# Planning the bit moves of pairs 6 and 7 at every other step of a fused attention and MLP kernel

## The chip, the cores and the metric

One core of a Trainium2 chip. The metric is the device time of one launch in microseconds (us). In a profile, times count from the first instruction of the span; a span is somewhat shorter than the device time (302.6 us for a run of 304.4 us). In the lines of a profile PE is TensorE, PEld its weight loads, DVE VectorE, ACT ScalarE and POOL GpSimd; L470 is line 470 of the kernel, x4 a count of instructions, and <- in brackets names what ended a wait.

## The reference, cut to what matters

```python
# attention with a hash mask: q, k, v are [4, 8, 768, 64], proj is [64, 6]
q_bits = (q @ proj > 0); k_bits = (k @ proj > 0)      # 6 bits per row
mask = bucket(q_bits) == bucket(k_bits)               # attend only within a bucket
attn = softmax(where(mask, q @ k.T / 8, -1e9))
x = (attn @ v)                                        # to [3072, 512]
# then an MLP: w_in [512, 2048], w_out [2048, 512]
h = x @ w_in
out = (h * sigmoid(h)) @ w_out
```

## The kernel before: the parts that matter

The kernel walks the 32 heads as 16 pairs, in 288 steps (nine score tiles per head), and slips the MLP of one batch element between the attention steps of the next. The bits of a pair are laid under its q and k rows, in tiles `QKA` (first head) and `QKB` (second head), so that a score matmul adds the mask by itself. The bits are computed for two pairs at once (`proj_unit`) and then moved to their rows (`bits_unit`), by VectorE for pairs up to 7 and by DMA above:

```python
def bits_unit(pairs, i, par):               # i: which pair, par: 0 = QKA, 1 = QKB
    p = pairs[i]
    t, r0 = ((QKA[p % NSL], 64), (QKB[p % NSL], 0))[par]
    if p > 7:
        ...                                 # DMAs
        return
    for n in range(2):                      # q rows, then k rows
        c = 32 * (2 * i + n)
        r = slice(c, c + NR)                # 13 partitions of the bits tile
        dst = t[r0 : r0 + NR, n * S : (n + 1) * S]...
        if n == 1 and par == 1:
            nc.vector.tensor_scalar(out=dst, in0=bits[pairs][r, :, 0:CB], ...)
        else:
            nc.vector.tensor_copy(out=dst, in_=bits[pairs][r, :, 0:CB])
```

So a group of moves is two VectorE instructions, and pairs 6 and 7 have four groups. The other user of VectorE that counts here is `g`, the last step of the first MLP matmul. Three PSUM tiles with the tag "m" rotate; a tile is free again when its `g` is done:

```python
hp = ps.tile([P, f, n], F32, tag="m", name="h_ps", bufs=3)
...                                         # four matmuls into hp
th = thp.tile([P, f, n], F32, tag="th", name="th")
nc.scalar.activation(out=th, in_=hp, func=AF.Tanh, scale=0.5)
after.append(lambda: nc.vector.scalar_tensor_tensor(    # g = (th + 1) * hp
    out=g[ci][...], in0=th, scalar=1.0, in1=hp, op0=ALU.add, op1=ALU.mult))
```

Each step issues the waiting `g` first, then what is planned for the step (`plan(step, fn)`), then MLP units and attention:

```python
for w in range(NW):
    flush()                                 # the g of the step before
    for fn in at.pop(w, []):
        fn()                                # planned units, such as bits_unit
    ...                                     # MLP units, av(w), score(w + LEAD)
```

Of the kernel before, what the change touches and what calls it, by code (L numbers as in the profile page):

```python
# [17 lines left out]
def kernel(  # L18
# [67 lines left out]
    def load_blocks(p):  # L86
        b, h0 = p // 4, 2 * (p % 4)
        for n, src in (("q", q), ("k", k)):
            t = ld.tile([P, NG, 32], F32, tag=f"ld{n}", name=f"{n}_blk")
            for j in range(4):  # L90
                i, half = divmod(j, 2)
                nc.sync.dma_start(  # L92
                    out=t[32 * j : 32 * j + 32],
                    in_=src[b, h0 + i].rearrange("(r g) d -> r g d", r=32)
                    [:, :, 32 * half : 32 * half + 32])
            qk_sb[p, n] = t

    def load_v(p, heads=slice(0, 2)):
        b, h0 = p // 4, 2 * (p % 4)
        if p not in v_sb:  # L100
            v_sb[p] = vld.tile([P, 2, NJ * D], F32, tag="ldv", name="v_sb")
        nc.sync.dma_start(
            out=v_sb[p][:, heads],
            in_=v[b, h0 : h0 + 2][heads].rearrange("h (p t) d -> p h (t d)", p=P))
# [135 lines left out]
    def block_unit(p, n):  # L240
        if n == 0:
            qk32[p] = t32.tile([P, 2 * S], F32, tag="qk32", name="qk32")

        dst = qk32[p][:, n * S : (n + 1) * S].rearrange(
            "p (t r a) -> p a t r", t=NJ, r=32, a=4)
        nc.vector.transpose(out=dst, in_=qk_sb[p, "qk"[n]])  # L246

    def cast_unit(p, par):
        sl = p % NSL
        dst, rows = ((QKA[sl], slice(0, 64)), (QKB[sl], slice(64, 128)))[par]  # L250
        nc.gpsimd.tensor_scalar(out=dst[rows, :], in0=qk32[p][rows, :],  # L251
                                scalar1=CS, scalar2=1.0,
                                op0=ALU.mult, op1=ALU.mult)

    def v_unit(p, heads=(0, 1)):
        for i in heads:
            h = 2 * p + i
            vv, vs = VV[h % NVS], VS[p % (NVS // 2)]
            src = v_sb[p][:, i, :].rearrange("p (t d) -> p t d", d=D)
            nc.gpsimd.tensor_copy(out=vv[:, :, 0:D], in_=src)  # L260
            sa = nrm.tile([P, 3, D], F32, tag="vsa", name="vsa")
            nc.gpsimd.tensor_tensor(out=sa, in0=src[:, 0:3], in1=src[:, 3:6], op=ALU.add)  # L262
            sb = nrm.tile([P, D], F32, tag="vsb", name="vsb")
            nc.gpsimd.tensor_tensor(out=sb, in0=sa[:, 0], in1=sa[:, 1], op=ALU.add)
            nc.gpsimd.tensor_tensor(out=vs[:, i, 0:D], in0=sb, in1=sa[:, 2], op=ALU.add)
# [4 lines left out]
    def proj_unit(*pairs):  # L270



        bt = btp.tile([P, 3, CB + 2], F16, tag="bits", name="bits")
        bps = []
        for c0, w in ((0, 512), (512, S - 512)):
            bp = ps.tile([P, 512], F32, tag="m", name="bp_ps", bufs=3)
            for i, p in enumerate(pairs):
                for n in range(2):
                    c = 32 * (2 * i + n)  # L280
                    nc.tensor.matmul(bp[c : c + 32, 0:w], pw[:, 0:32],  # L281
                                     qk32[p][:, n * S + c0 : n * S + c0 + w],
                                     start=True, stop=True)
            bps.append((bp, c0, w))
        r = slice(0, 64 * len(pairs))
        for bp, c0, w in bps:
            nc.vector.tensor_scalar(out=bt[r, c0 // CB : (c0 + w) // CB, 0:CB],
                                    in0=bp[r, 0:w].rearrange("d (x c) -> d x c", c=CB),
                                    scalar1=sc[r, 0:1], scalar2=sc[r, 1:2],
                                    op0=ALU.is_gt, op1=ALU.subtract)  # L290
        bits[pairs] = bt
# [30 lines left out]
    def bits_unit(pairs, i, par):  # L322
# [5 lines that stand above are left out]
            o = par * (NBIT + 1)  # L328
            for n in range(2):
                r = 32 * (2 * i + n) + o  # L330
                nc.sync.dma_start(out=t[r0 + o : r0 + o + NBIT, n * S : (n + 1) * S]
                                  .rearrange("d (x c) -> d x c", c=CB),
                                  in_=bits[pairs][r : r + NBIT, :, 0:CB])
            return
        for n in range(2):
            c = 32 * (2 * i + n)
            r = slice(c, c + NR)
            dst = t[r0 : r0 + NR, n * S : (n + 1) * S].rearrange("d (x c) -> d x c", c=CB)
            if n == 1 and par == 1:
                nc.vector.tensor_scalar(out=dst, in0=bits[pairs][r, :, 0:CB],  # L340
                                        scalar1=sc[r, 2:3], scalar2=None, op0=ALU.mult)
            else:
                nc.vector.tensor_copy(out=dst, in_=bits[pairs][r, :, 0:CB])  # L343
# [228 lines left out]
    def plan(w, fn):  # L572
        at.setdefault(w, []).append(fn)
# [35 lines left out]
    for Q in range(2, NQUAD):  # L609
        w0 = (Q - 1) * QST  # L610
        for i in range(4 if Q > 2 else 0):
            w1 = w0 + (5, 9, 12, 15)[i]
            plan(w1, lambda Q=Q, i=i: block_unit(2 * Q + i // 2, i % 2))
            if i % 2:
                for par in range(2):
                    plan(w1, lambda p=2 * Q + i // 2, par=par: cast_unit(p, par))
        wp = w0 + {2: 24, 3: 21}.get(Q, 20)
        plan(wp, lambda Q=Q: proj_unit(2 * Q, 2 * Q + 1))
        for i in range(4):
            plan(wp + (i if Q < 4 else 0),  # L620
                 lambda Q=Q, i=i: bits_unit((2 * Q, 2 * Q + 1), i // 2, i % 2))
        for i in range(2):
            plan(w0 + 5 + i, lambda p=2 * Q + i: load_v(p))
            for j in range(2):
                plan(w0 + 18 + 9 * i + 2 * j, lambda p=2 * Q + i, j=j: v_unit(p, (j,)))
            if Q + 1 < NQUAD:
                plan(w0 + (28 if Q == 3 else 8) + i, lambda p=2 * Q + 2 + i: load_blocks(p))
# [74 lines left out]
```

## Time and profile before

| kernel before | value |
|---|---|
| device time, median of 4 runs (lowest, highest) | 304.20 us (304.14, 304.9) |
| span of the profiled run | 302.6 us |
| busy: TensorE, ScalarE, VectorE, GpSimd | 98%, 69%, 59%, 42% |
| visible waits of h_ps matmuls for g, all together | 0.8 us, one wait |

TensorE sets the time. The question for any change of VectorE's order is therefore whether TensorE waits for VectorE anywhere, and for how long.

### The profile page before, as it was taken

The page shows a single profiled execution, that of the slowest core. Times are in us where ns is not written, and L with a number is a line of the kernel's source. Part 1 is how long each engine was busy: PE and PEld are TensorE (multiplying, and loading weights), DVE is VectorE, ACT ScalarE, POOL GpSimd, SP SyncE. Part 2 cuts the span into 40 slices and gives each one's busy share as a digit, 9 for nine tenths or more (in the row PEclk, how much of TensorE's full clock was granted, in tenths as well). Part 3 has the DMA queues.
Part 4 walks back from the last instruction along what each step waited for, and adds up shares of the span by engine and source line. Part 5 has one row for each costly group of instructions (what it writes and reads, how often), then busy time and mean ns, then how long its engine had stood idle before and what let it go on. Part 6 is the DMA issues. An engine that isn't in the chain of part 4 may idle for free.

```text
span 302.6 us, 7181 instructions
## 1 busy us (share of the span) xinstructions
PE 297.0 (98%) x2710; PEld 175.1 (58%) x2710; DVE 180.0 (59%) x344; ACT 210.1 (69%) x392; POOL 128.2 (42%) x203
## 2 busy tenths in 40 slices
PE   8999999998999999999999999999999999999996
PEld 3676755545665665555565665555566654446653
DVE  5797938899568454854695434954443442764332
ACT  5987989988887686878886766878877732452300
POOL 6589999386618561845149411765111100000000
PEclk9999999999999999999999999999999999999999
DMA  7999998999979828744068146011022003001112
GB/s 202 245 248 215 156 145 122 217 180 166 145 161 153 131 74 229 124 97 134 3 126 139 51 63 203 2 40 32 2 61 63 4 34 95 35 2 69 37 66 73
DMA packets 103170, 32.87 MB, mean 109 GB/s; under 512 B 90656, under 2 KB 100192, under 8 KB 103136
## 3 DMA queue, kind: packets, MB, share of 16 engines
q1 hardware_dynamic: 98752, 28.22, 43.3%
q0 software_dynamic: 4224, 4.19, 9.0%
q8 instruction: 21, 0.34, 0.5%
q14 instruction: 13, 0.11, 0.1%
q10 hardware_dynamic: 160, 0.00, 0.0%
HBM read 27.27 MB, written 6.29 MB: 111 GB/s over the span
## 4 chain that ended last, share of the span: by engine, by line
PE 89%; DVE 5%; DMA 2%; issue 1%; SPq 1%; ACT 1%; POOL 0%; DVEq 0%; ACTq 0%; POOLq 0%
PE o_ps L496 26%; PE h_ps L461 24%; PE s_ps L366 18%; PE o_ps L398 11%; PE bp_ps L281 3%; DMA v_sb<-in_v_dram 2%; PE tp_ps L185 2%; DVE g L470 2%; PE o_ps L482 1%; PE warm_ps L125 1%; SPq L92 1%; DVE qka L343 1%; PE bp_ps L225 1%; DVE qk L246 1%; PE tp_ps L198 0%
## 5 line engine op out<-in xcount | busy, mean ns | idle before, releaser
L369 ACT ACTIVATE u<-s_ps 128x512 f16<-128x512 f32 x288 | 157.0, 606 | 38.7 <-PE s_ps L366 38.3
L470 DVE SCALAR_TENSOR_TENSOR g<-th,h_ps 128x512 f16<-128x512 f32 x96 | 65.5, 686 | 74.8 <-ACT th L468 74.7
L461 PE MATMUL h_ps<-xT,win 128*128 128x512 f16 (+1 forms) x512 | 98.4, 325 | 0.8 <-DVE g L470 0.8
L398 PEld LDWEIGHTS <-u 128*128 128x128 f16 x1152 | 68.1, 98 | 42.2 <-ACT u L369 8.4
L496 PE MATMUL o_ps<-wout,g 128*128 128x512 f16 x368 | 91.6, 379 | 0.0
L468 ACT ACTIVATE th<-h_ps 128x512 f32<-128x512 f32 x96 | 57.9, 603 | 36.6 <-PE h_ps L461 33.9
L398 PE MATMUL o_ps<-vv,u 128*128 128x65 f16 x1152 | 82.6, 194 | 0.6 <-ACT u L369 0.4
L461 PEld LDWEIGHTS <-win 128*128 128x128 f16 x512 | 49.8, 98 | 31.4 <-issue 1.0
L418 POOL TENSOR_TENSOR x_pr<-osum,rec 128x384 f16<-128x384 f32 x23 | 19.0, 826 | 89.3 <-DVE rec L417 88.9
L496 PEld LDWEIGHTS <-g 128*128 128x128 f16 x368 | 35.8, 98 | 33.6
L366 PE MATMUL s_ps<-qka 71*128 71x512 f16 x192 | 52.7, 327 | 0.2 <-DVE qka L238 0.2
L366 PE MATMUL s_ps<-qkb 128*128 128x512 f16 x192 | 52.6, 326 | 0.0
L251 POOL TENSOR_SCALAR qka<-qk 64x1536 f16<-64x1536 f32 x15 | 22.0, 1466 | 11.4 <-DVE qk L246 5.6
L501 DVE TENSOR_SCALAR osb<-o_ps 128x512 f32<-128x512 f32 x23 | 15.9, 691 | 15.0 <-PE o_ps L496 15.0
L251 POOL TENSOR_SCALAR qkb<-qk 64x1536 f16<-64x1536 f32 x15 | 22.1, 1471 | 1.2
L262 POOL TENSOR_TENSOR vsa<-v_sb 128x192 f32<-128x192 f32 x32 | 19.0, 592 | 0.0
L260 POOL CAST vv<-v_sb 128x384 f16<-128x384 f32 x32 | 16.2, 507 | 0.9 <-DMA v_sb<-in_v_dram 0.5
L246 DVE STREAM_TRANSPOSE qk<-k_blk 128x768 f32<-128x768 f32 x10 | 15.8, 1582 | 0.3 <-issue 0.3
L246 DVE STREAM_TRANSPOSE qk<-q_blk 128x768 f32<-128x768 f32 x10 | 15.9, 1591 | 0.0
L366 PEld LDWEIGHTS <-qka 71*128 71x128 f16 x192 | 15.5, 97 | 0.8 <-ACT qka L238 0.7
L366 PEld LDWEIGHTS <-qkb 128*128 128x128 f16 x192 | 15.4, 97 | 0.0
L412 DVE TENSOR_TENSOR osum<-o_ps,vsum 128x390 f32<-128x390 f32 x23 | 13.0, 565 | 2.3
(70 smaller groups left out, 163.0 us busy)
## 6 DMA issues: line engine op xcount, KB each, us to landing
out_dram<-osb SPq DMA_DIRECT2D x23, 256.0 KB
v_sb<-in_v_dram SPq DMA_DIRECT2D x15, 384.0 KB
q_blk<-in_q_dram SPq DMA_DIRECT2D x40, 96.0 KB
k_blk<-in_k_dram SPq DMA_DIRECT2D x40, 96.0 KB
win<-in_moe_w_in_dram POOLq DMA_DIRECT2D x4, 512.0 KB, 6.6
wout<-in_moe_w_out_dram POOLq DMA_DIRECT2D x4, 512.0 KB, 6.9
q_sb<-in_q_dram SPq DMA_DIRECT2D x5, 384.0 KB
k_sb<-in_k_dram SPq DMA_DIRECT2D x5, 384.0 KB
```

The lines of the kernel that those rows point to most:

```text
L246: nc.vector.transpose(out=dst, in_=qk_sb[p, "qk"[n]])
L251: nc.gpsimd.tensor_scalar(out=dst[rows, :], in0=qk32[p][rows, :], scalar1=CS, scalar2=1.0, op0=ALU.mult, op1=ALU.mult)
L260: nc.gpsimd.tensor_copy(out=vv[:, :, 0:D], in_=src)
L262: nc.gpsimd.tensor_tensor(out=sa, in0=src[:, 0:3], in1=src[:, 3:6], op=ALU.add)
L366: nc.tensor.matmul(sp[:, o0 : o0 + n], t[rows, S + jt * P : S + (jt + 1) * P], t[rows, c0 : c0 + n], start=True, stop=True)
L369: nc.scalar.activation(out=u, in_=sp, func=AF.Exp, scale=ESC)
L398: nc.tensor.matmul(o_ps[h][:, c0 // P + i, :], u[:, o0 + i * P : o0 + (i + 1) * P], vv[:, jt, :], start=(not direct(h) and w % NU == 0 and ...
L418: (nc.vector if direct(h) else nc.gpsimd).tensor_tensor(out=x_pr[p][:, :, par * D : (par + 1) * D], in0=o[:, 0:NJ, 0:D], in1=rec[:, :, Non ...
L461: nc.tensor.matmul(hp[:, j, :], w_in16[:, dt, ft * P : (ft + 1) * P], xT[4 * b + dt][:, c0 : c0 + n], start=(dt == 0), stop=(dt == NDT - 1))
L468: nc.scalar.activation(out=th, in_=hp, func=AF.Tanh, scale=0.5)
L470: after.append(lambda: nc.vector.scalar_tensor_tensor(out=g[ci][:, grp * f : (grp + 1) * f, :], in0=th, scalar=1.0, in1=hp, op0=ALU.add, o ...
L496: nc.tensor.matmul(o2[tt], g[ci][:, ft, ct * P : (ct + 1) * P], w_out16[:, ft, :], start=(ft == 0), stop=(ft == NFT - 1))
```

## The change

The intent is to let the `g` instructions of the MLP pass between the moves. Only the steps of the four groups of pairs 6 and 7 (Q = 3) change, from 93, 94, 95, 96 to 93, 95, 97, 99:

```diff
         for i in range(4):
-            plan(wp + (i if Q < 4 else 0),
+            plan(wp + {2: i, 3: 2 * i}.get(Q, 0),
                  lambda Q=Q, i=i: bits_unit((2 * Q, 2 * Q + 1), i // 2, i % 2))
```

## The prediction

> **What bounds the kernel now.** I read the summary of the page first, then the sum of waits of the whole run, then the chain that ended last around the steps that the change touches, and last the order in time of TensorE and VectorE there.
>
> ```profile
> PE 297.0 (98%) x2710; PEld 175.1 (58%) x2710; DVE 180.0 (59%) x344; ACT 210.1 (69%) x392; POOL 128.2 (42%) x203
> PE h_ps L461 <- DVE g L470: 0.8, 1, 0.8
> ```
>
> The first line is the busy time of each engine: TensorE is busy for 297.0 of 302.6 us. The second is from the list of waits: of all the matmuls that write the hidden tile h_ps of the second half (the MLP), exactly one waits visibly for VectorE, once, for 0.8 us. So a change that only reorders VectorE can win little more than that one gap. The other VectorE work is mostly beside TensorE.
>
> The chain that ended last shows where the gap is. Columns: start, length, what.
>
> ```profile
> 67.09 1.18 DVE bits L287 x2
> ...
> 68.30 0.54 DVE qka L343
> ...
> 68.86 0.54 DVE qka L343
> ...
> 69.42 0.54 DVE qkb L343
> ...
> 69.97 0.60 DVE qkb L340
> ...
> 70.60 0.69 DVE g L470
> ...
> 71.32 0.54 DVE qka L343
> ...
> 73.00 0.61 DVE qkb L340
> ...
> 73.64 0.70 DVE g L470
> 74.33 0.04 issue
> 74.38 1.02 PE h_ps L461 x4
> ```
>
> The reader is to see that from 67.09 to 74.33 us the chain runs through VectorE: eight bit moves (two groups of four) with one g between and one behind them, and that it then passes to TensorE, where it stays, but for short waits near 97 us, to the last output tile. L343 and L340 are the two forms of a bit move; these are the moves of pairs 6 and 7, the ones the change replans. L470 makes g from th and h_ps and so frees the PSUM tile of h_ps.
>
> TensorE and VectorE in order of time, in the same place (start, length, what, idle before):
>
> ```profile
> 71.83 1.03 PE L461 MATMUL h_ps<-xT,win 128*128 128x512 f16 x4
> ...
> 73.16 0.38 PE L366 MATMUL s_ps<-qkb 128*128 128x256 f16 x2
> 74.38 1.02 PE L461 MATMUL h_ps<-xT,win 128*128 128x512 f16 x4 [0.84 <-DVE g L470]
> ...
> 75.97 1.04 PE L461 MATMUL h_ps<-xT,win 128*128 128x512 f16 x4
> ```
> ```profile
> 74.24 0.22 DVE L411 COPY vsum<-o_ps 128x65 f32<-128x65 f32 x1
> ...
> 75.27 1.84 DVE L470 SCALAR_TENSOR_TENSOR g<-th,h_ps 128x512 f16<-128x512 f32 x3
> 77.68 0.69 DVE L470 SCALAR_TENSOR_TENSOR g<-th,h_ps 128x512 f16<-128x512 f32 x1 [0.57 <-ACT th L468]
> ```
>
> I number the h_ps tiles by their start on TensorE: H1 67.51, H2 69.09, H3 70.63, H4 71.83, H5 74.38, H6 75.97, H7 77.56. The pool has three buffers, so H5 needs the g of H2. That g was runnable at 70.75 (its tanh starts at 70.15 and takes 0.60), but VectorE takes its work in order and did it only at 73.64 to 74.33. H5 starts 0.05 later. A score pair such as the one at 73.16 is normally followed 0.22 us later by the next tile (69.95 to 70.07 to 70.29 and so on), so H5 should have started at 73.38: by starts the stall is 74.38 - 73.38 = 1.00 us; the 0.84 is counted from the modelled end of the matmul. H6 lost a further 0.06: due 0.22 after the score at 75.69, it started at 75.97, 0.05 after the first g of the three at 75.27. In all 1.06 us is there to be won.
>
> **What the Trainium skill says.** "PSUM — Partial Sum Buffer", section "Engine vs sequencer instructions": the queues of VectorE, ScalarE and GpSimd are strictly first in, first out, and matmuls start and complete in program order. The trace agrees: H2's g, runnable at 70.75, stands behind four moves until 73.64, and no TensorE work passes H5. "Perfetto Trace Analysis", section "Matmuls": independent groups should rotate through PSUM banks so that the evacuation of one overlaps the matmuls of the next. Here they do, with three tiles, and the rotation breaks just once, by 1.00 us. "VectorE: DVE Perf Modes", section "Two Vector instructions with no wait between them": in its model, an instruction whose operands start at another group of 32 partitions than the last ones waits for all earlier ones. The trace agrees: g after g starts every 0.59 us though each takes 0.69 (59.11 and three in 1.84), while a g after a bit move, or a move after a g, starts 0.02 to 0.03 us after its end. So each g that the change puts between moves loses about 0.1 us of overlap that a row of g has.
>
> **The change part by part.** It adds and removes no instruction. For pairs 6 and 7 the four groups of moves (two instructions each) are planned at steps 93, 95, 97, 99 in place of 93 to 96. The built program shows TensorE, ScalarE, GpSimd and the DMA issues in the same order as before; only a few VectorE instructions change places. Before: A A B B, g1, A' A' B' B', g2, the normalization (vsum, osum, rec), g3, g4, g5. After: A A, g1, B B, g2, A' A', normalization, g3, B' B', g4, g5. A is the copy into qka of pair 6, B the moves into qkb, the dash is pair 7. The deadline is far off: the first score of pair 6 is issued at step 105 and of pair 7 at 123.
>
> Replay of VectorE with the pitches from the trace (move 0.56, the L340 form to a g 0.63, g to move 0.72, vsum to the g behind rec 1.03, g to g 0.59):
> - A A at 68.30 and 68.86, as before. g1 at 69.42 (its tanh ends at 69.17), before 70.60.
> - B B at 70.14 and 70.70, g2 at 71.32, done 72.01 in place of 74.33. H5 wants it at 73.38, so H5 no longer waits: 1.37 us of slack. This is the whole win: H5 starts 1.00 earlier.
> - A' A' at 72.04 and 72.60, vsum at 73.16 (its last matmul comes at 71.49 and ends before), g3 at 74.19, done 74.88. H6 is now due at 73.38 + 1.53 = 74.91 and can start at 74.93: it loses 0.02.
> - B' B' at 74.91 and 75.47, g4 at 76.10, done 76.79. H7 needs g4. It is due 1.59 after H6 (77.56 - 75.97), at 76.52, and can start at 76.84. Here the change gives back 0.32.
> - g5 follows at 76.69 and ends at 77.38; the next user of the rotation, the output tile that started at 79.11, now comes at 78.39. No wait. After that VectorE has idle time before its g, as it had.
>
> The sum: H7 starts at 76.84 in place of 77.56, so 1.06 - 0.02 - 0.32 = 0.72 us is won. From there the chain is TensorE in the same order, and what it still waits for near 97 us (tanh, g, then the projection) hangs on TensorE's own work and moves with it. VectorE, ScalarE and GpSimd busy times do not change. 304.26 - 0.72 = 303.54, so 303.5 us.
>
> **The rivals.** First, the wait moves and is not removed: moves at steps 97 and 99 now stand ahead of g3 and g4, and TensorE reaches these sooner. My replay already has 0.32 us of this; if each held start cost 0.1 us more than I read, H6 and H7 would each lose more and the win would shrink to 0.4 or 0.5 (303.8). For it speaks that the slack at H6 is nil; against it that the idle time of VectorE right behind, 0.57 at 77.68, stops it spreading. Second, ScalarE takes over: in steps with a tanh and two exps every 1.55 us it works without a pause (th at 68.57, 70.15 and 71.69, each with two exps behind it), and in the 0.84 us gap it caught up, with 0.97 us idle at 75.44. With TensorE running on, the exps could come late by 0.1 to 0.3. The three-deep score buffers speak against more; the time would be 303.6 to 303.8. Third, the full 1.06 is kept, if B' B' ends earlier than I think or H7's wait hides in a weight load: 303.2. Fourth, nothing: a transfer or the slow end of the loads sets a later point in absolute time, and 304.2 stays. Against it: no TensorE wait on a DMA stands in the list of waits, and buffers free up sooner when TensorE is sooner.
>
> **Range and chances.** The three runs before lie at 304.14, 304.26 and 304.9, so the median of a few runs can be off by about 0.2. The mechanisms span 303.2 to 304.2. Hence 303.1 to 304.2, with 303.5 in it. Two per cent is 6.1 us, nearly six times all that the gap can give, and a loss of that size would need a new wait of seven times the one that is there; so within 2% has a chance of 0.99, and the rest is split.
>
> **What would show it right or wrong.** In the profile after: no 0.84 gap ahead of the fifth h_ps group, which starts near 73.4; H2's g starts near 71.3; a smaller new wait of H7 for g, about 0.3 us near 76.8; the wait "h_ps for g" in the list falls below 0.4 in all; TensorE's tiles after 80 us all about 0.7 us earlier; other engines' counts and durations as before. I am wrong if H5 still waits for g, if the gap turns up at ScalarE's exps or at H7 at full size, or if the tiles after 80 us are earlier and the end is not.

## The result, and the profile after

The changed kernel took 303.38 us (median of 4 runs, 303.11 to 303.9) against 304.20 us, so 0.82 us less by the medians. The ratio of the two is 0.997, with a 95% interval of 0.995 to 0.999: clear of 1. Ratios here and below are the mean time of one kernel's runs over that of the other's of the same rounds, so they are not quite the ratio of the medians that are quoted.

The summary line of engines in the page after: the counts of instructions are the same, and no busy time differs by more than 0.4 us. What the change does can't be seen in such sums.

```profile
PE 296.6 (98%) x2710; PEld 175.1 (58%) x2710; DVE 180.1 (60%) x344; ACT 210.1 (70%) x392; POOL 128.3 (43%) x203
```

VectorE of the changed kernel in order of time (start, length, line, what). H1 to H7 name the h_ps tiles as in the prediction, and g1 to g5 their g:

```profile
67.84 1.10 DVE L343 COPY qka<-bits 13x768 f16<-13x768 f16 x2
68.97 0.69 DVE L470 SCALAR_TENSOR_TENSOR g<-th,h_ps 128x512 f16<-128x512 f32 x1
69.58 0.53 DVE L343 COPY qkb<-bits 13x768 f16<-13x768 f16 x1
...
70.76 0.69 DVE L470 SCALAR_TENSOR_TENSOR g<-th,h_ps 128x512 f16<-128x512 f32 x1
71.48 1.10 DVE L343 COPY qka<-bits 13x768 f16<-13x768 f16 x2
...
73.65 0.65 DVE L470 SCALAR_TENSOR_TENSOR g<-th,h_ps 128x512 f16<-128x512 f32 x1
74.33 0.54 DVE L343 COPY qkb<-bits 13x768 f16<-13x768 f16 x1
...
75.53 1.88 DVE L470 SCALAR_TENSOR_TENSOR g<-th,h_ps 128x512 f16<-128x512 f32 x3
```

The g at 70.76 is g2. Two moves stand ahead of it since g1, no longer four. TensorE in the same place:

```profile
71.37 1.03 PE L461 MATMUL h_ps<-xT,win 128*128 128x512 f16 x4
...
72.92 1.03 PE L461 MATMUL h_ps<-xT,win 128*128 128x512 f16 x4
...
74.45 1.03 PE L461 MATMUL h_ps<-xT,win 128*128 128x512 f16 x4
...
75.81 0.38 PE L366 MATMUL s_ps<-qkb 128*128 128x512 f16 x1
76.27 1.02 PE L461 MATMUL h_ps<-xT,win 128*128 128x512 f16 x4
```

H4 to H7 start at 71.37, 72.92, 74.45 and 76.27. No line carries a wait in brackets. But H7 comes 0.46 after the score at 75.81, where 0.22 is the normal distance: it waits 0.24 us by this count (0.23 against e5_pair7_late below, where it doesn't wait). The list of waits doesn't show it, as it counts idle time from the modelled end of the matmul before (75.81 + 0.38 = 76.19). The chain that ended last does: it goes from VectorE to TensorE at just this point.

```profile
75.53 0.70 DVE g L470
76.22 0.04 issue
76.27 1.02 PE h_ps L461 x4
```

All times of this trace are 0.46 us early already at H1 (67.05, before 67.51), ahead of anything that the change touches. So I compare distances within a trace, from H1 on:

| from H1, us | before | after |
|---|---|---|
| to H5 | 6.87 | 5.87 |
| to H6 | 8.46 | 7.40 |
| to H7 | 10.05 | 9.22 |
| to the last output group (o_ps, L482) | 228.79 | 227.96 |
| from H7 to that group | 218.74 | 218.74 |

The last two rows take the start of the group from the chain of each kernel, first before, then after:

```profile
296.30 3.51 PE o_ps L482 x32
```
```profile
295.01 3.51 PE o_ps L482 x32
```

H5 gains 1.00 us, H6 a further 0.06, H7 gives back 0.23, and the 0.83 us that are left reach the end undiminished: from H7 to the last group both kernels take 218.74 us. The two spans differ by 1.3 us, but 0.46 us of that was there before the change began.

### The profile page after: what moved, and what is told of

The parts are those of the page before. It is cut to its first block, busy times and chain, and to the rows that moved or that the text cites. A ratio compares the mean times of both kernels' runs of the same rounds, so it can differ in the third digit from the quotient of the medians.

```text
span 301.3 us, 7181 instructions
## 1 busy us (share of the span) xinstructions
PE 296.6 (98%) x2710; PEld 175.1 (58%) x2710; DVE 180.1 (60%) x344; ACT 210.1 (70%) x392; POOL 128.3 (43%) x203
## 4 chain that ended last, share of the span: by engine, by line
PE 88%; DVE 7%; DMA 1%; ACT 1%; issue 1%; SPq 1%; DVEq 0%; ACTq 0%
PE o_ps L496 26%; PE h_ps L461 24%; PE s_ps L366 19%; PE o_ps L398 12%; DVE g L470 3%; PE bp_ps L281 3%; PE tp_ps L185 2%; DMA k_row<-in_k_dram 1%; PE o_ps L482 1%; DVE qk L246 1%; DVE qka L343 1%; ACT u L369 1%; DVE osum L412 1%; SPq L79 0%; PE o_ps L389 0%
```

## The experiments

Each is told by the edit against the changed kernel, if not said otherwise. All outputs were correct. Here are all of them by distance from H1, beside the timed runs ("before" is the control of the same chip, 11 runs):

| run | H1 to H5 | H1 to H7 | H7 to last group | median us (range) | control | ratio, 95% interval |
|---|---|---|---|---|---|---|
| e1_as_changed | 5.87 | 9.22 | 218.74 | 303.05 (303.03 to 303.75) | 304.27 | 0.9967, 0.9955 to 0.9979 |
| e2_all_at_once | 7.67 | 10.79 | 218.74 | 305.00 (304.72 to 305.27) | 304.27 | 1.0024, 1.0012 to 1.0036 |
| e3_pair6_only | 6.74 | 9.93 | 218.75 | 303.94 (303.83 to 305.07) | 304.27 | 0.9996, 0.9984 to 1.0008 |
| e4_pair7_only | 5.87 | 9.20 | 218.74 | 303.52 (303.1 to 304.53) | 304.27 | 0.9985, 0.9972 to 0.9998 |
| e1b_as_changed | 5.87 | 9.22 | 218.74 | 303.51 (303.33 to 305.02) | 304.25 | 0.9978, 0.9957 to 0.9999 |
| e5_pair7_late | 5.87 | 8.99 | 218.74 | 303.02 (302.88 to 303.65) | 304.25 | 0.9959, 0.9944 to 0.9973 |
| e6_by_dma | 5.87 | 8.98 | 218.81 | 303.73 (302.96 to 305.32) | 304.25 | 0.9984, 0.9961 to 1.0007 |
| e7_qkb_first | 5.87 | 9.22 | 218.74 | 303.31, one run | | |

**The change again.** No edit.

> The changed kernel again, beside its control. My theory (the g of H2 stood behind four moves; TensorE wins 1.06 us at H5 and H6 and gives back about 0.23 at H7): 0.8 us faster than the kernel before, H5 to H1 5.87 us by starts in place of 6.87, H7 to H1 about 9.2 in place of 10.05. Rival (the gain is chance in how a run starts, since the profiled run was 0.46 us ahead already at H1): the times of the two kernels overlap and the ratio is 1.000 within its interval.

The ratio of 0.9967 lies clear of 1, and every distance is the one of the first trace to the hundredth. The rival (chance) falls: the gain stays though this profiled run's H1 came at 67.36, 0.31 us later than in the first.

**All four groups at once.**

```diff
-            plan(wp + {2: i, 3: 2 * i}.get(Q, 0),
+            plan(wp + {2: i, 3: 0}.get(Q, 0),
```

> All four groups of moves of pairs 6 and 7 at step 93, so eight moves in a row ahead of g1. My theory: g1 is done 5.3 us after the first move starts, H4 (three tiles after H1) starts about 1.8 us late, H5 to H7 don't wait, H7 to H1 is 10.8 us, the time 0.8 us over the kernel before (305.0). Rival (VectorE's total backlog counts, not its order): as before, 304.2, since the same eight moves and the same g are done by the same time.

TensorE and then VectorE of this run:

```profile
70.50 1.03 PE L461 MATMUL h_ps<-xT,win 128*128 128x512 f16 x4
73.51 1.02 PE L461 MATMUL h_ps<-xT,win 128*128 128x512 f16 x4 [1.65 <-DVE g L470]
```
```profile
72.13 0.61 DVE L340 TENSOR_SCALAR qkb<-bits,sc 13x768 f16<-13x768 f16 x1
72.77 1.29 DVE L470 SCALAR_TENSOR_TENSOR g<-th,h_ps 128x512 f16<-128x512 f32 x2
```

With eight moves in a row, g1 starts only at 72.77, and now H4 waits for it: H1 to H4 is 6.13 us, in place of 4.32 before. Nobody waits after that, and the time is 305.00 us. VectorE does the same work in each of these kernels, yet here it costs 0.74 us more than before and 1.57 more than the change (229.53 from H1 to the last group, against 228.79 and 227.96). The rival, that only the backlog counts, falls.

**Only pair 6 spread.**

```diff
-            plan(wp + {2: i, 3: 2 * i}.get(Q, 0),
+            plan(wp + {2: i, 3: (0, 2, 2, 3)[i]}.get(Q, 0),
```

> Half of the change: only the second group of pair 6 goes one step later (steps 93, 95, 95, 96). My theory: g1 comes earlier, but six moves now stand ahead of g2, which ends about 5.85 us after the first move as against 6.0; H5 still waits, some 0.15 us less; time 0.1 us under the kernel before (304.1). Rival (any spreading of the moves helps in proportion): half of the gain, 0.4 us, 303.8.

```profile
74.06 1.02 PE L461 MATMUL h_ps<-xT,win 128*128 128x512 f16 x4 [0.71 <-DVE g L470]
```

H5 still waits, by 0.13 us less than before (6.74 against 6.87), and H1 to H7 is 0.12 shorter. The timed ratio of 0.9996 tells this neither from nothing nor quite from half of the gain (0.4 us would be 0.9987, just inside the interval); the trace decides it. Half of the spreading does not bring half of the gain.

**Only pair 7 later.**

```diff
-            plan(wp + {2: i, 3: 2 * i}.get(Q, 0),
+            plan(wp + {2: i, 3: (0, 1, 4, 6)[i]}.get(Q, 0),
```

> The other half: pair 6 at steps 93 and 94 as before, pair 7 at 97 and 99 as in the change. My theory: g1 comes as late as before, which nobody waits for, g2 follows it at once, about 3.6 us after the first move; H5 and H6 don't wait, H7 waits about 0.2; the whole gain of 0.8 us, 303.4. Rival (spreading helps in proportion): 0.4 us, 303.8.

```profile
69.50 0.60 DVE L340 TENSOR_SCALAR qkb<-bits,sc 13x768 f16<-13x768 f16 x1
70.13 1.29 DVE L470 SCALAR_TENSOR_TENSOR g<-th,h_ps 128x512 f16<-128x512 f32 x2
71.45 1.10 DVE L343 COPY qka<-bits 13x768 f16<-13x768 f16 x2
```

The two in the second line are g1 and g2, one straight after the other. The four moves of pair 6 ahead of g1 harm nobody; H1 to H7 is 9.20 us, even 0.02 less than with the whole change, so here too it is the trace that decides: the timed ratio of 0.9985, with its interval, would fit the rival's 0.4 us as well. The part of the change that counts is that pair 7's moves no longer stand between g1 and g2.

**The change once more, as a neighbour of the next ones.**

> The changed kernel once more, as the neighbour of the next two on the same chip. 0.8 us faster than the kernel before; the wait of H7 for g 0.2 to 0.25 us by starts.

The same distances a third time. The timed runs spread over 1.7 us, more than the effect; what the traces show of the reason is at the end of this section.

**Pair 7 behind the crowd.**

```diff
-            plan(wp + {2: i, 3: 2 * i}.get(Q, 0),
+            plan(wp + {2: i, 3: (0, 2, 12, 14)[i]}.get(Q, 0),
```

> Pair 6 as in the change, pair 7's moves at steps 105 and 107, behind g3 and g4 in VectorE's order, where VectorE has idle time; their deadline is step 123. My theory: nobody waits from H4 to H7, H7 to H1 is 8.98 us, so 0.2 us more than the change wins, 1.0 to 1.1 us under the kernel before (303.1). Rival (ScalarE takes over once VectorE is out of the way): H7 is late all the same behind the tanh and exps, and the time equals that of the change.

```profile
72.56 1.35 DVE L470 SCALAR_TENSOR_TENSOR g<-th,h_ps 128x512 f16<-128x512 f32 x2
74.77 0.69 DVE L470 SCALAR_TENSOR_TENSOR g<-th,h_ps 128x512 f16<-128x512 f32 x1 [0.86 <-ACT th L468]
76.30 0.69 DVE L470 SCALAR_TENSOR_TENSOR g<-th,h_ps 128x512 f16<-128x512 f32 x1 [0.85 <-ACT th L468]
77.02 1.10 DVE L343 COPY qka<-bits 13x768 f16<-13x768 f16 x2
```

The first line is g3 and g4; then VectorE is idle until g5, and again until g6, and the moves of pair 7 come behind. H7 no longer waits: H1 to H7 is 8.99 us, 1.06 us less than before, all that the prediction counted as there to be won. The range of the timed runs lies under every one of the 11 control runs (303.8 the lowest). That it also beats the change, by 0.23 us, is read from the trace; the timed runs of the two overlap. That ScalarE would take over (the rival) falls too.

**The moves by DMA.** Against the kernel before:

```diff
-        if p > 7:
+        if p > 5:
```

> The kernel before, with the moves of pairs 6 and 7 taken off VectorE and given to DMAs, as it does for pairs 8 and up. My theory: the eight moves are gone from the queue, VectorE is 4.5 us less busy, H7 to H1 is 8.98 us, the time 1.0 to 1.1 us under the kernel before, the same as with pair 7 late. Rival (VectorE's load, not its order, costs time elsewhere too): more than that, by 0.3 us and over. Second rival: the DMA issues delay loads behind them in the same queue and something waits for these: no gain.

H1 to H7 is 8.98 us, within 0.01 of the run above, and VectorE is 4.1 us less busy (175.9), not 4.5: with the eight moves gone altogether, VectorE's lighter load brings nothing beyond the 1.06 us. From H7 on this kernel alone takes 0.07 us more. TensorE where that arises:

```profile
108.56 0.28 PE L398 MATMUL o_ps<-vv,u 128*128 128x65 f16 x4
108.75 0.38 PE L366 MATMUL s_ps<-qka 71*128 71x512 f16 x1
```

The second line is the first score that reads bits which a DMA moved. It starts 0.19 us after the group ahead of it; in the kernel before it took 0.12 (109.11 to 109.23). So the first rival falls by the trace, and for the second (a load held up) TensorE shows no gap of another kind. Why this score starts 0.07 late was not tried. It is not a cost of every such move: in the trace of the kernel before, where pairs 8 and up get their bits by DMA, none of the 192 scores that follow such a group after 66 us stands more than 0.14 us behind it. From H1 to the last group this kernel takes 227.79 us, 1.00 less than before. By time alone, 0.9984 with an interval that holds 1, this run is inconclusive: the medians give 0.5 us, not the 1.0 to 1.1 expected.

**The two groups of a pair swapped.** This tests the distance from a g to a move, the term of my sum that was off:

```diff
-                 lambda Q=Q, i=i: bits_unit((2 * Q, 2 * Q + 1), i // 2, i % 2))
+                 lambda Q=Q, i=i: bits_unit((2 * Q, 2 * Q + 1), i // 2, (i + (Q == 3)) % 2))
```

> The changed kernel with the two groups of each pair swapped: qkb moves first, qka second. It tests the term that I sized wrong: a move behind a g starts 0.61 us after it where it starts at the same partitions (into qkb, from bits of pair 6), and 0.68 to 0.72 where it starts at others. Now all moves behind g but none of pair 6 into qkb change places: both qka groups stand behind a g or a rec and start at partition 64. My theory: each g to move distance is 0.68 to 0.72 us, and H7's wait is 0.3 us in place of 0.23. Rival (the distance is chance or set by the bits tile): 0.61 shows up again behind g1 and H7's wait stays 0.23.

```profile
69.25 0.69 DVE L470 SCALAR_TENSOR_TENSOR g<-th,h_ps 128x512 f16<-128x512 f32 x1
69.97 1.10 DVE L343 COPY qka<-bits 13x768 f16<-13x768 f16 x2
...
72.37 0.61 DVE L340 TENSOR_SCALAR qkb<-bits,sc 13x768 f16<-13x768 f16 x1
72.91 0.20 DVE L411 COPY vsum<-o_ps 128x65 f32<-128x65 f32 x1
...
73.92 0.65 DVE L470 SCALAR_TENSOR_TENSOR g<-th,h_ps 128x512 f16<-128x512 f32 x1
74.60 1.10 DVE L343 COPY qka<-bits 13x768 f16<-13x768 f16 x2
```

Half a miss. The distances came as said: g1 to the move is now 0.72 us, where it was 0.61 (68.97 to 69.58), and g3 to the move is 0.68. But H7's wait did not grow; H1 to H7 stays 9.22. The reason is in the middle lines: vsum now follows a move into qkb, whose output rows start at partition 0 like its own (its input, o_ps, is in PSUM, which no move reads), and starts 0.54 after it though that takes 0.61, so it overlaps. e5_pair7_late, where vsum also follows a move into qkb, shows the same (79.43 to 79.97). In the changed kernel it followed a move into qka, whose rows start at 64, and did not (72.03 + 0.55, vsum at 72.61). The swap costs one overlap and gains another: from the first move to g4 it is 7.68 us here (75.74 - 68.06) and 7.69 in the changed kernel (75.53 - 67.84). I had counted the distances behind g and forgotten the other one.

**Why single runs scatter by a microsecond.** H1 lies between 67.03 and 68.03 us in the ten traces, though the kernels order the work up to there alike. The second bit projection of the first pair (L225) shows where that comes from. TensorE before, then in the repeat of the change with the late H1 (67.99):

```profile
5.71 0.97 PE L225 MATMUL bp_ps<-qk,pw 128*32 128x384 f32 x8
9.82 0.85 PE L225 MATMUL bp_ps<-qk,pw 128*32 128x384 f32 x8
```
```profile
5.66 1.50 PE L225 MATMUL bp_ps<-qk,pw 128*32 128x384 f32 x8
10.30 0.85 PE L225 MATMUL bp_ps<-qk,pw 128*32 128x384 f32 x8
```

From the second of these to H1 it is 67.51 - 9.82 = 57.69 us and 67.99 - 10.30 = 57.69 us; in all ten traces it is 57.68 to 57.70. All scatter of H1 is made in the first 10 us, and the spans of the three traces of the changed kernel less their H1 agree to 0.1 us (234.2 to 234.3). For runs without a trace the same is likely, but not shown. In the pair above nothing waits longer: the eight matmuls of the first group are slower, each 0.84 to 0.85 us where the kernel before has 0.49 to 0.64. e6_by_dma, the other trace with H1 near 68, shows this too (0.85); the other eight don't. In three of the early ones (after, e4, e5; H1 67.03 to 67.20) the chain that ended last runs through the load of k_row instead. No experiment was made on this. In this kernel 0.8 us is more surely read from one trace, as a distance, than from five timed runs.

## Why the prediction was right

- **The place and the bound.** Right. TensorE waited for g once, for the g of H2, and the time moved by what that wait was worth. H1 to H5 was forecast as 73.38 - 67.51 = 5.87 and measured as 5.87.
- **The win of 1.06 us.** Right: 1.00 at H5 and 0.06 at H6, and e5_pair7_late, which takes the later wait away as well, reached 1.06 in full. Which moves were in the way, the prediction did not separate; e3 and e4 showed that pair 7's did, and pair 6's did not.
- **H6 loses 0.02.** It lost nothing (7.40 from H1, just its due distance of 5.87 + 1.53).
- **H7 gives back 0.32.** The mechanism was right and the size off: 0.23. The term that was mis-sized is the step from g to move, 0.72, which I took from the one example in the trace and used for all. Measured it is 0.61 behind g1, where move and g start at the same partitions, 0.72 behind g2 and 0.68 behind g3, which itself takes 0.65 and not 0.69. The three steps are 0.15 us shorter than I had them, and the other steps of the replay 0.04 longer in sum, so g4 comes 7.69 us after the first move and not 76.10 - 68.30 = 7.80. The 0.11 are the whole difference between the forecast 9.33 (76.84 - 67.51) and the measured 9.22. The rule of the page that I quoted would have told me: I wrote down that a change of partitions holds an instruction back, and then let the first move into qkb of pair 6, which reads bits from partition 0, pay for it where nothing changed. (The pitch of 0.59 from g to g was also read a little high: the two places named for it give 1.25 - 0.69 = 0.56 and (1.84 - 0.69) / 2 = 0.575. No step up to H7 rests on it.)
- **The chain behind H7 moves as it is.** Right: 218.74 us in both.
- **The sum.** Forecast gain 0.72 us, by the trace 0.83, by the medians 0.82; forecast 303.5, measured 303.38, in the range. That the medians come so near to the trace is luck: the two repeats of the same change give 1.22 us (304.27 - 303.05) and 0.74 us (304.25 - 303.51).
- **The rivals.** "The wait moves" was right in kind and smaller than feared. ScalarE did not take over (e5). "The full 1.06 is kept" was not so for the change, but was for e5. "Nothing" fell in each of the repeats.

## What to carry to other kernels

On an engine that takes its work in order, look for the short jobs with a far deadline that stand ahead of a job that somebody waits for, and move those, as far as their deadline allows; here it mattered less how many there were in all than which of them stood between the job and its turn. A stretch that is just unblocked reaches the next buffer sooner, so replay the next two or three users as well: here the second wait took back 0.23 of 1.06 us, and planning pair 7's moves eight steps later than the change does kept it. For gains below the scatter of runs, measure the distance between two events of one trace that enclose the change.

## What the Trainium skill lacked or had wrong

- "VectorE: DVE Perf Modes", section "Two Vector instructions with no wait between them": the rule was borne out (e7 moved the overlaps just where the start partitions said), but the section gives no cost. Here a held move starts 0.68 to 0.72 us after a g of 0.65 to 0.69, one that isn't held 0.61: about 0.1 us each.
- "Perfetto Trace Analysis", section "Summary: the profiler window per engine type", says that a matmul's profiled end is an estimate. No run here shows the true end. What the section does not say is that a wait read from these ends comes out too small: a score of 0.38 us is normally followed after 0.22 us, so the list has 0.84 for 1.00 us at H5 before, and nothing for the 0.23 us at H7 after.
